# Score tiles of pooled attention as 64-row products in two halves of the TensorE array, with K's copies exchanged between the halves

## The chip, the cores and the metric

One core of one Trainium2 chip. The metric is the device time of one execution in microseconds (us); the number shown for a kernel is the median of several runs. PE is TensorE's product side, PEld its weight loads, DVE VectorE, ACT ScalarE, POOL GpSimd and SP SyncE, which issues the DMAs.

## What is computed

```python
q_pool = q.reshape(B, H, S // 2, 2, D).mean(axis=3)          # B 2, H 8, S 1152, D 64
scores = q_pool @ k.transpose(0, 1, 3, 2) / sqrt(D)
attn = softmax(scores)                                       # 576 x 1152 per head
x = concat_heads(attn @ v)                                   # 1152 x 512
out = sum_e p[:, e:e+1] * (relu(x @ w1[e]) @ w2[e])          # 4 experts, hidden 1024
```

All is float32. To stay near that accuracy with the faster fp32r products, the kernel splits an operand into hi (rounded to fp32r) and lo (the rest), and sums three terms: hi·hi, hi·lo and lo·hi.

## The kernel before

The attention stage works on eight pairs of heads, `n` = 0 to 7. A pair has nine score tiles `i` of 128 pooled queries by 1152 keys: tile `i` below 8 belongs to head `h = i % 2`, tile 8 holds the last 64 queries of both. The program is one hand-written order: block `g = 9n + i` issues, in this order on PE,

- the 18 transposes of the finished tile `g` (`T_chunk`, `pt`, 64 rows at a time, through `half_transposes` at L202),
- a part of the products with V of an older group (`PV_part`, `po`, L376),
- in some blocks a further transposition: `pr` in blocks 2 and 7 (`spread_sums`, which spreads the inverse row sums), `pk` in blocks 1 and 3 (`prep_k`, half of the next pair's K), `pq` in block 8 (`prep_q`, the q of the pair after next),
- the scores of tile `g + 3` (`S_rows`, or `S_chunk` for tile 8 and for pair 0), into a PSUM buffer of three banks of which there is one (`ps_s`). DVE sweeps it at L341 (scale, minimum, copy to SBUF), and only then may the next tile's scores be written.

From pair 1 on, tiles 0 to 7 go through `S_rows` (56 tiles). `q2` holds q hi (`z` = 0) and q lo (`z` = 1) of each head, the same in both halves of the 128 partitions. `kab` holds K of head 0 in rows 0 to 63 and of head 1 in rows 64 to 127, hi and lo apart. `k2[:, h]` holds hi and lo of head `h` one above the other, so that a 128-row product gives hi·hi + hi·lo at once. `S_rows` issues three such products at L334 (512, 512 and 128 columns), and then the lo·hi term as three 64-row products at L338: columns 0 to 511 in the upper row half, 512 to 1023 in the lower, 1024 to 1151 in the upper.

K of the pair ahead comes by these steps: the load into `kn` (L173, block 3), `join_k` on POOL (L262), which puts the two heads side by side in `kc`, transposes (`pk`), a copy to `raw` on DVE or ACT, `pool_split` on POOL (L209 hi, L210 lo) into `kab`, and `stack_k` (L274), four DMAs per call from `kab` to `k2`. `join_k(0)` stands in block 6, `join_k(1)` at the end of `prep_q` in block 8, `join_k(2)` in `prep_k`. POOL also splits the finished attention output (`finish`) and q (`prep_q`), in one queue.

After attention the expert stage runs 128-row products (L135 and L710) on 16 weight slices; the change does not touch it, save that its first products begin inside pair 7's blocks 7 and 8.

Of the kernel before, what the change touches and what calls it, by code (L numbers as in the profile page):

```python
# [8 lines left out]
F32 = mybir.dt.float32  # L9
# [8 lines left out]
def attention_moe_kernel(ctx, tc, q, k, v, probs, w1, w2, out):  # L18
    nc = tc.nc
# [3 lines left out]
    P = 128  # L23
    HALF = 64
# [11 lines left out]
    ident = const.tile([P, P], F32, name="ident")  # L36
# [18 lines left out]
    k2 = [t[:, :2 * S].rearrange("p (h s) -> p h s", h=2) for t in kk]  # L55
    kab = [t[:, 2 * S:].rearrange("p (z s) -> p z s", z=2) for t in kk]
    khl = kk[1][:, 2 * S:].rearrange("p (h t z d) -> p h t z d", h=2, t=KT, z=2)
    q2 = [q2all[:, :2304], q2all[:, 3328:]]
    stq = q2all[:, 2304:3328].rearrange("p (z s j x) -> p z s j x", z=2, s=2, j=4)
    q2m = [t[:, 2048:].rearrange("p (z x) -> p z x", z=2) for t in q2]  # L60
    q2 = [t[:, :2048].rearrange("p (z s x) -> p z s x", z=2, s=2) for t in q2]
# [77 lines left out]
    ps_t = ctx.enter_context(tc.tile_pool(name="ps_t", bufs=2, space=PSUM))  # L139
# [3 lines left out]
    with ExitStack() as actx:  # L143
# [6 lines left out]
        rb = [ap.tile([P, w], F32, name=f"rb{i}") for i, w in enumerate(GW)]  # L150
        raw = ap.tile([P, 7 * P], F32, name="raw")
        spread = ap.tile([P, 4 * HALF], F32, name="spread")
# [3 lines left out]
        pr = ap.tile([P, 2 * 9, E], F32, name="pr")  # L156
# [7 lines left out]
        NP = len(pairs)  # L164
# [27 lines left out]
        ROWS = [slice(0, HALF), slice(HALF, P)]  # L192

        def half_transposes(name, blocks, pool=None):
            if pool is None:
                pt = ps_t.tile([P, 2, 512], F32, tag="t", name=name)
            else:
                pt = pool.tile([P, 3, 512], F32, tag="s", name=name)[:, :2]
            pt = pt[:, :, :len(blocks) * HALF].rearrange("p a (k x) -> p a k x", x=HALF)
            for j, src in enumerate(blocks):  # L200
                for a, r in enumerate(ROWS):
                    nc.tensor.transpose(pt[:, a, j, :], src[r], ident[r, r])  # L202
            return pt

        def halves(t, t0, t1):
            return t[:, t0 * P:t1 * P].rearrange("p (k a x) -> p a k x", a=2, x=HALF)
# [26 lines left out]
        def half_of(h, z):  # L233
            return z if h else 1 - z
# [25 lines left out]
        def join_k(c):  # L260
            t0, t1 = KTS[c]
            nc.gpsimd.tensor_copy(  # L262
                kc[c].rearrange("p (t h d) -> p t h d", h=2, d=D), kn[:, :, t0:t1].rearrange("p h t d -> p t h d"))
# [4 lines left out]
            pool_split(ab[:, 0, cols], ab[:, 1, cols], src)  # L268

        def stack_k(n, t0, t1):  # L270
            cols, ab = slice(t0 * P, t1 * P), kab[n % 2]
            for h in range(2):
                for z in range(2):
                    nc.sync.dma_start(  # L274
                        k2[n % 2][ROWS[half_of(h, z)], h, cols].bitcast(F32), ab[ROWS[h], z, cols].bitcast(F32))

        def prep_q(n):
            pt = half_transposes("pq", [qsum[:, 2 * j:2 * j + 2].rearrange("p t d -> p (t d)") for j in range(5)] + [kc[0]])
            src = raw[:, :6 * P].rearrange("p (a k x) -> p a k x", a=2, x=HALF)
            nc.scalar.activation(src, pt, AF.Copy)  # L280
            pool_split(stq[:, 0], stq[:, 1], src[:, :, :4])
            for y in range(2):
                for half in range(2):
                    r = slice(half * HALF, (half + 1) * HALF)
                    dst = q2[n % 2].rearrange("p z s (y x) -> p (z s) y x", y=2)[r, :, y, :]
                    st = stq.rearrange("p z s j x -> p (z s) (j x)")[y * HALF:(y + 1) * HALF]
                    nc.sync.dma_start(dst.bitcast(F32), st.bitcast(F32))
            split_q2m(n, src)
            ab = kab[n % 2]
            pool_split(halves(ab[:, 0], 8, 9)[:, :, 0], halves(ab[:, 1], 8, 9)[:, :, 0], src[:, :, 5])  # L290
            if n > 1:
                join_k(1)

        def prep_k(n, c):
            t0, t1 = KTS[c]
# [17 lines left out]
        def S_chunk(g, c):  # L313
# [9 lines left out]
            for j, (w, x) in enumerate(ops):  # L323
                nc.tensor.matmul(spt[g][:, c], w, x, start=(j == 0), stop=(j == len(ops) - 1))  # L324

        def S_rows(g):
            n, i = tiles[g]
            t, h = divmod(i, 2)
            ts_ = slice(t * P, (t + 1) * P)
            sp = ps_s.tile([P, 3, 512], F32, tag="s", name="spt").rearrange("p a b -> p (a b)")[:, :S]  # L330
            spt[g] = sp.rearrange("p (c x) -> p c x", c=3)
            cs = [slice(0, 512), slice(512, 1024), slice(1024, S)]
            for c in cs:
                nc.tensor.matmul(sp[:, c], q2[n % 2][:, 0, h, ts_], k2[n % 2][:, h, c], start=True, stop=False)  # L334
            hi = [kab[n % 2][:, 0, :], k2[n % 2][:, h]]
            for a, c in ((0, cs[0]), (1, cs[1]), (0, cs[2])):
                r = ROWS[a]
                nc.tensor.matmul(sp[:, c], q2[n % 2][r, 1, h, ts_], hi[(a + h) % 2][r, c], start=False, stop=True)  # L338

        def neg_scores(g):  # L340
            nc.vector.tensor_scalar(  # L341
# [46 lines left out]
                spread.rearrange("p (c x) -> p c x", x=HALF), r[:, :4].unsqueeze(2).to_broadcast([P, 4, HALF]))  # L388

        def spread_sums(n, grp):  # L390
            pt = ps_t.tile([P, 2, 512], F32, tag="t", name="pr")[:, 0]
            r = rs[n % 2][:, 4 * grp:]
            for j in range(2):
                nc.tensor.transpose(pt[:, j * P:(j + 1) * P], spread[:, j * P:(j + 1) * P], ident)
            if grp:
                nc.tensor.transpose(pt[:, 2 * P:3 * P], r[:, 4:5].to_broadcast([P, P]), ident)
            nc.vector.tensor_copy(rb[grp][:, :256], pt[:, :256])
            if grp:
                for a, h in enumerate(ROWS):
                    nc.vector.tensor_copy(rb[1][h, 256:], pt[h, 256 + a * HALF:256 + (a + 1) * HALF])  # L400

        def split_x(op, kt, c, src, eng):
            hi, lo = xop(op, 0, kt)[:, c], xop(op, 1, kt)[:, c]
# [121 lines left out]
        for g in range(NTL):  # L525
            n, i = divmod(g, 9)
            if i == 4 and 0 < n and n + 1 < NP:
                load_kv(vn[(n + 1) % 2], v, n + 1)
            if i == 6 and n + 2 < NP:
                add_q(nc.gpsimd)  # L530
                join_k(0)
            if i == 2 and n + 2 < NP:
                load_q(n + 2)
            if g == NTL - 1:
                nc.scalar.activation(UT["m1"], chx[:, :2, :CW], AF.Copy)
            for c in range(2):
                T_chunk(g, c)
            if g <= NQT:
                exps(g + 1)
            if i == 0 and n:  # L540
                inv_sums(n - 1, 1)
            if i == 4:
                inv_sums(n, 0)
            if g == NTL - 1:
                inv_sums(n, 1)
            if NQT < g < NTL - 2 and i not in (3, 8):
                exps(g + 2)
            if g == NQT:
                PV_part(0, 1, 0, 1)
                scores(g + 2)  # L550
                exps(g + 2)
                PV_part(0, 1, 1, 3)
            else:
                pv_part(g)
            if i in SPREAD and n + SPREAD[i][0] >= 0:
                spread_sums(n + SPREAD[i][0], SPREAD[i][1])
            if g == 0:
                prep_q0()
            if n + 1 < NP:
                for fn, *args in (PREP if n else PREP0).get(i, []):  # L560
                    fn(n + 1, *args)
                if i == 8 and n + 2 < NP:
                    prep_q(n + 2)
                if i == (3 if n else 5) and n + 2 < NP:
                    load_kv(kn, k, n + 2)
            elif i == 7:
                chx = ps_s.tile([P, 3, 512], F32, tag="s", name="chx")
                for kt in range(2):
                    product(0, 0, kt, chx, True)
            elif i == 8:  # L570
                for kt in range(2):
                    product(0, 2, kt, chx, False)
            if NQT <= g < NTL - 2 and i in (3, 8):
                exps(g + 2)
            scores(g + 2 if g < NQT else g + 3)
            if g == 0:
                stack_k0()
                add_q(nc.gpsimd)
                join_k(0)
                join_k(1)  # L580
            if (n, i) == (1, 4):
                gate_weights()
            if (n, i) == (NP - 2, 4):
                load_w1(0)
            if (n, i) == (NP - 2, 7):
                w1_sums(0)
            if n == NP - 1:
                if i == 0:
                    split_x("S3", 1, slice(0, HT), xr[:, 1, :HT], nc.gpsimd)
                    load_w2(0)  # L590
                if i < 4:
                    w1_hi(0, WCH[i:i + 1])
                    w1_lo(0, WCH[i:i + 1])
                if i == 3:
                    load_w1(1)
                if i == 5:
                    w1_sums(1)
# [156 lines left out]
```

## Time and profile before

| | |
|---|---|
| median of 3 runs (lowest to highest) | 633.5 us (633.44 to 633.63) |
| the profiled execution: its own time, its span | 633.96 us, 632.1 us |
| PE busy in the span | 615.0 us (97%) |
| share of the chain that ended last on PE | 80% |
| score products, L334 and L338 (busy) | 53.2 us and 40.3 us |
| attention stage up to pair 7's last products with V | 0 to 247 us |
| chain through the expert stage's second products, L710 | 31% |

The busy times of L334 and L338 are 40.8 + 12.4 us and 28.0 + 12.3 us, 512-column and 128-column products. Busy times of PE overlap, since each product's end is modelled: its real rate is read from the starts of successive products, not from the lengths. In the timelines, neighbouring instructions of one line are merged into one row: its start is that of the first, and the start of the next row tells when the work after it began.

### The profile page before, as it was taken

The page shows a single profiled execution, that of the slowest core. Times are in us where ns is not written, and L with a number is a line of the kernel's source. Part 1 is how long each engine was busy: PE and PEld are TensorE (multiplying, and loading weights), DVE is VectorE, ACT ScalarE, POOL GpSimd, SP SyncE. Part 2 cuts the span into 40 slices and gives each one's busy share as a digit, 9 for nine tenths or more (in the row PEclk, how much of TensorE's full clock was granted, in tenths as well). Part 3 has the DMA queues.
Part 4 walks back from the last instruction along what each step waited for, and adds up shares of the span by engine and source line. Part 5 has one row for each costly group of instructions (what it writes and reads, how often), then busy time and mean ns, then how long its engine had stood idle before and what let it go on. Part 6 is the DMA issues. An engine that isn't in the chain of part 4 may idle for free.

```text
span 632.1 us, 12010 instructions
## 1 busy us (share of the span) xinstructions
PE 615.0 (97%) x4828; PEld 504.1 (80%) x4828; DVE 367.5 (58%) x571; ACT 293.9 (46%) x467; POOL 346.8 (55%) x415
## 2 busy tenths in 40 slices
PE   7899999999999999999999999999999999999997
PEld 6666666666666666889889989989989989989976
DVE  6667777777777777654454454454454454454454
ACT  5656666666666674544135135135235235235120
POOL 1654454453545498694485485485476476476040
PEclk8999999999999999999999999999999999999999
DMA  7655373736454510121121121121121121120105
GB/s 229 142 156 147 111 177 111 204 88 180 99 157 102 146 35 17 51 67 35 35 66 34 34 67 34 33 68 35 33 67 35 34 66 34 39 63 1 35 0 150
DMA packets 41783, 50.88 MB, mean 80 GB/s; under 512 B 3712, under 2 KB 27520, under 8 KB 41728
## 3 DMA queue, kind: packets, MB, share of 16 engines
q1 hardware_dynamic: 40928, 48.94, 28.0%
q10 hardware_dynamic: 800, 1.18, 0.5%
q8 instruction: 38, 0.62, 0.4%
q14 instruction: 17, 0.14, 0.1%
HBM read 30.97 MB, written 2.36 MB: 53 GB/s over the span
## 4 chain that ended last, share of the span: by engine, by line
PE 80%; POOL 8%; DVE 4%; issue 3%; ACT 2%; DMA 1%; SPq 0%; POOLq 0%; DVEq 0%; ACTq 0%
PE p L710 31%; PE chy L135 11%; PE chz L135 8%; PE chx L135 7%; PE po L376 7%; PE spt L334 4%; PE pt L202 4%; PE spt L338 3%; PE spt L324 2%; POOL q2all L210 2%; DVE sx L341 1%; DMA kq<-in_k_dram 1%; POOL q2all L209 1%; POOL xb L408 1%; PE pk L202 1%
## 5 line engine op out<-in xcount | busy, mean ns | idle before, releaser
L710 PE MATMUL p<-w2s,hb 128*128 128x512 f32 (+1 forms) x870 | 199.2, 388 | 1.1 <-DVE acc L714 0.9
L710 PEld LDWEIGHTS p<-w2s,hb 128*128 128x128 f32 x870 | 161.7, 188 | 34.3 <-issue 1.3
L714 DVE SCALAR_TENSOR_TENSOR acc<-p,pw,acc 128x512 f32<-128x512 f32 (+1 forms) x136 | 101.6, 747 | 82.7 <-PE p L710 82.7
L116 POOL TENSOR_TENSOR kk<-kq,kk 128x512 fp32r<-128x512 f32 x64 | 72.5, 1162 | 117.8 <-ACT kk L108 117.8
L341 DVE TENSOR_SCALAR_CACHE_REDUCE sx<-spt 128x1152 f32<-128x1152 f32 x72 | 97.7, 1358 | 57.7 <-PE spt L338 34.3
L347 ACT ACTIVATE sx<-sx,mn 128x1152 f32<-128x1152 f32 x72 | 90.5, 1257 | 23.6 <-DVE sx L341 23.5
L376 PE MATMUL po<-aT,vn 128*64 128x320 f32 (+1 forms) x576 | 85.5, 418 | 0.0
L641 POOL TENSOR_TENSOR hb<-xr,hb 128x576 fp32r<-128x576 f32 x48 | 68.7, 1434 | 21.9 <-ACT hb L640 21.8
L678 ACT ACTIVATE xr<-chx 128x576 f32<-128x576 f32 x15 | 9.8, 652 | 147.5 <-PE chx L135 147.5
L363 ACT ACTIVATE aT<-pt 128x640 f32<-128x640 f32 x72 | 50.6, 702 | 40.6 <-PE pt L202 40.6
L202 PEld LDWEIGHTS pt<-ident,sx 64*128 64x128 f32 x1296 | 53.8, 140 | 7.8 <-issue 3.4
L135 PE MATMUL chx<-xa,kk 128*128 128x288 f32 x384 | 56.4, 296 | 0.8 <-ACT xr L678 0.4
L202 PE MATMUL pt<-ident,sx 64*128 64x64 f32 x1296 | 56.5, 225 | 0.5 <-ACT xr L302 0.4
L135 PEld LDWEIGHTS chx<-xa,kk 128*128 128x128 f32 x384 | 53.4, 188 | 2.8 <-ACT xr L678 0.7
L376 PEld LDWEIGHTS po<-aT,vn 128*64 128x64 f32 x576 | 35.0, 136 | 20.1 <-issue 0.5
L361 DVE COPY aT<-pt 128x512 f32<-128x512 f32 x72 | 49.4, 686 | 2.4 <-PE pt L202 2.4
L95 POOL TENSOR_TENSOR kq<-kq 128x256 f32<-128x256 f32 x64 | 45.8, 738 | 7.7 <-DMA kq<-in_moe_w_dram 6.4
L639 ACT ACTIVATE xr<-xr 128x576 f32<-128x576 f32 x48 | 32.9, 686 | 34.0 <-DVE xr L637 33.9
L135 PE MATMUL chy<-xb,kk 128*128 128x288 f32 x288 | 46.6, 297 | 0.3 <-ACT xr L647 0.2
L334 PE MATMUL spt<-kk,q2all 128*128 128x512 f32 x168 | 44.1, 370 | 0.9 <-DVE sx L341 0.9
L135 PE MATMUL chy<-q2all,kk 128*128 128x288 f32 x256 | 44.1, 294 | 0.0
L617 POOL TENSOR_TENSOR w2s<-qsf,w2s 128x512 fp32r<-128x512 f32 x32 | 40.7, 1292 | 3.1 <-ACT w2s L615 3.1
(107 smaller groups left out, 757.4 us busy)
## 6 DMA issues: line engine op xcount, KB each, us to landing
kq<-in_moe_w_dram SPq DMA_DIRECT2D x64, 128.0 KB, 2.4
qsf<-in_moe_w_dram SPq DMA_DIRECT2D x16, 512.0 KB, 3.6
q2all<-q2all SPq DMA_DIRECT2D x28, 256.0 KB, 4.3
vn<-in_v_dram SPq DMA_DIRECT2D x8, 576.0 KB, 5.4
kk<-kk SPq DMA_DIRECT2D x28, 160.0 KB, 2.7
kq<-in_q_dram SPq DMA_DIRECT2D x7, 576.0 KB, 3.9
kq<-in_k_dram SPq DMA_DIRECT2D x7, 576.0 KB, 4.4
kk<-kk SPq DMA_DIRECT2D x28, 128.0 KB, 2.9
```

Of the source, the lines that this page charges most:

```text
L116: nc.gpsimd.tensor_tensor(flat(w1s[u % 2][:, 1, a:b]), flat(wf[:, a:b]), flat(w1s[u % 2][:, 0, a:b].bitcast(F32)), ALU.subtract)
L135: nc.tensor.matmul(chain[:, c, :CW], w1s[u % 2][:, a, WI[wo], kt, :], xop(xo, z, kt)[:, c * CW:(c + 1) * CW], start=(first and kt == 0 and ...
L202: nc.tensor.transpose(pt[:, a, j, :], src[r], ident[r, r])
L334: nc.tensor.matmul(sp[:, c], q2[n % 2][:, 0, h, ts_], k2[n % 2][:, h, c], start=True, stop=False)
L341: nc.vector.tensor_scalar(sx[g % 3].rearrange("p (c x) -> p c x", c=3), spt.pop(g), -INV, None, ALU.mult, ALU.min, accum_out=mn[g % 3])
L347: nc.scalar.activation(sx[g % 3], sx[g % 3], AF.Exp, bias=mn[g % 3], scale=-1.0, accum_out=sums[n % 2][:, i:i + 1])
L361: nc.vector.tensor_copy(dst, pt)
L363: nc.scalar.activation(dst, pt, AF.Copy)
L376: nc.tensor.matmul(po[h * HALF:(h + 1) * HALF, :w], vn[n % 2][:, h, kt, :], aT[grp][:, h, kt, :], start=(kt == 0), stop=(kt == KT - 1))
L641: nc.gpsimd.tensor_tensor(lo, c, hi.bitcast(F32), ALU.subtract)
L710: nc.tensor.matmul(pc, h[:, a, sl, ts_], w[:, b, sl, c0:c1], start=(m == 0), stop=(m == len(ops) - 1))
L714: nc.vector.scalar_tensor_tensor(ac, pc, pw[:, tt, e:e + 1], ac, ALU.mult, ALU.add)
```

## The change

- `S_rows` makes all three terms as 64-row products: for each term one in the upper half (columns 0 to 511) and one in the lower (512 to 1023), then the three terms of columns 1024 to 1151 in the upper half. Each column part has its own PSUM bank. Nine products a tile in place of six.
- `k2` becomes `kab` with the two row halves exchanged, so that each head's K lies in both halves: `kab` where `a == h`, `k2` elsewhere. `stack_k` issues two DMAs per call in place of four, with the same bytes; each now copies hi and lo together, and so waits for both.
- `spread_sums` uses `half_transposes`: four (blocks 7) or six (blocks 2) 64-row transposes in place of two or three 128-row ones.
- `join_k(1)` moves from the end of `prep_q` (block 8) to the start of block 7.

```diff
--- before.py
+++ after.py
@@ -268,11 +268,10 @@
             pool_split(ab[:, 0, cols], ab[:, 1, cols], src)
 
         def stack_k(n, t0, t1):
-            cols, ab = slice(t0 * P, t1 * P), kab[n % 2]
+            cols = slice(t0 * P, t1 * P)
             for h in range(2):
-                for z in range(2):
-                    nc.sync.dma_start(
-                        k2[n % 2][ROWS[half_of(h, z)], h, cols].bitcast(F32), ab[ROWS[h], z, cols].bitcast(F32))
+                nc.sync.dma_start(
+                    k2[n % 2][ROWS[1 - h], :, cols].bitcast(F32), kab[n % 2][ROWS[h], :, cols].bitcast(F32))
 
         def prep_q(n):
             pt = half_transposes("pq", [qsum[:, 2 * j:2 * j + 2].rearrange("p t d -> p (t d)") for j in range(5)] + [kc[0]])
@@ -288,8 +287,6 @@
             split_q2m(n, src)
             ab = kab[n % 2]
             pool_split(halves(ab[:, 0], 8, 9)[:, :, 0], halves(ab[:, 1], 8, 9)[:, :, 0], src[:, :, 5])
-            if n > 1:
-                join_k(1)
 
         def prep_k(n, c):
             t0, t1 = KTS[c]
@@ -323,6 +320,9 @@
             for j, (w, x) in enumerate(ops):
                 nc.tensor.matmul(spt[g][:, c], w, x, start=(j == 0), stop=(j == len(ops) - 1))
 
+        LANES = [(a, a, zq, zk) for zq, zk in ((0, 0), (0, 1), (1, 0)) for a in range(2)] + [
+            (0, 2, 0, 0), (0, 2, 0, 1), (0, 2, 1, 0)]
+
         def S_rows(g):
             n, i = tiles[g]
             t, h = divmod(i, 2)
@@ -330,12 +330,12 @@
             sp = ps_s.tile([P, 3, 512], F32, tag="s", name="spt").rearrange("p a b -> p (a b)")[:, :S]
             spt[g] = sp.rearrange("p (c x) -> p c x", c=3)
             cs = [slice(0, 512), slice(512, 1024), slice(1024, S)]
-            for c in cs:
-                nc.tensor.matmul(sp[:, c], q2[n % 2][:, 0, h, ts_], k2[n % 2][:, h, c], start=True, stop=False)
-            hi = [kab[n % 2][:, 0, :], k2[n % 2][:, h]]
-            for a, c in ((0, cs[0]), (1, cs[1]), (0, cs[2])):
+            for a, c, zq, zk in LANES:
                 r = ROWS[a]
-                nc.tensor.matmul(sp[:, c], q2[n % 2][r, 1, h, ts_], hi[(a + h) % 2][r, c], start=False, stop=True)
+                src = kab if a == h else k2
+                nc.tensor.matmul(
+                    sp[:, cs[c]], q2[n % 2][r, zq, h, ts_], src[n % 2][r, zk, cs[c]],
+                    start=(zq + zk == 0), stop=(zq == 1))
 
         def neg_scores(g):
             nc.vector.tensor_scalar(
@@ -388,16 +388,13 @@
                 spread.rearrange("p (c x) -> p c x", x=HALF), r[:, :4].unsqueeze(2).to_broadcast([P, 4, HALF]))
 
         def spread_sums(n, grp):
-            pt = ps_t.tile([P, 2, 512], F32, tag="t", name="pr")[:, 0]
             r = rs[n % 2][:, 4 * grp:]
-            for j in range(2):
-                nc.tensor.transpose(pt[:, j * P:(j + 1) * P], spread[:, j * P:(j + 1) * P], ident)
-            if grp:
-                nc.tensor.transpose(pt[:, 2 * P:3 * P], r[:, 4:5].to_broadcast([P, P]), ident)
-            nc.vector.tensor_copy(rb[grp][:, :256], pt[:, :256])
+            pt = half_transposes("pr", [spread[:, j * P:(j + 1) * P] for j in range(2)] + (
+                [r[:, 4:5].to_broadcast([P, P])] if grp else []))
+            nc.vector.tensor_copy(halves(rb[grp], 0, 2), pt[:, :, :2])
             if grp:
                 for a, h in enumerate(ROWS):
-                    nc.vector.tensor_copy(rb[1][h, 256:], pt[h, 256 + a * HALF:256 + (a + 1) * HALF])
+                    nc.vector.tensor_copy(rb[1][h, 256:], pt[h, a, 2])
 
         def split_x(op, kt, c, src, eng):
             hi, lo = xop(op, 0, kt)[:, c], xop(op, 1, kt)[:, c]
@@ -529,6 +526,8 @@
             if i == 6 and n + 2 < NP:
                 add_q(nc.gpsimd)
                 join_k(0)
+            if i == 7 and n + 2 < NP:
+                join_k(1)
             if i == 2 and n + 2 < NP:
                 load_q(n + 2)
             if g == NTL - 1:
```

What stands on PE from `pk` in block 1 to the scores in block 2 of a pair, before (`pt` transposes, `po` products with V, `pk` and `pr` as above, `spt` scores, x the count):

```order
L202 MATMUL pk<-ident,qsf 128x64 x8
L334 MATMUL spt<-kk_73,q2all 128x512 x2
L334 MATMUL spt<-kk_73,q2all 128x128
L338 MATMUL spt<-kk_73,q2all 128x512 x2
L338 MATMUL spt<-kk_73,q2all 128x128
L202 MATMUL pt<-ident,sx_92 128x64 x18
L376 MATMUL po<-aT_94,vn_89 64x320 x4
L394 MATMUL pr<-ident,spread 128x128 x2
L396 MATMUL pr<-ident,rs_105 128x128
L334 MATMUL spt<-kk_73,q2all 128x512 x2
```

and with the change:

```order
L202 MATMUL pk<-ident,qsf 128x64 x8
L336 MATMUL spt<-kk_73,q2all 128x512 x6
L336 MATMUL spt<-kk_73,q2all 128x128 x3
L202 MATMUL pt<-ident,sx_92 128x64 x18
L376 MATMUL po<-aT_94,vn_89 64x320 x4
L202 MATMUL pr<-ident,spread 128x64 x4
L202 MATMUL pr<-ident,rs_105 128x64 x2
L336 MATMUL spt<-kk_73,q2all 128x512 x6
L336 MATMUL spt<-kk_73,q2all 128x128 x3
```

The two shapes of score products, 128-row at L334 and 64-row at L338, have become one line of 64-row products, L336; and `pr` is now made by the line of the other transposes.

What stands on POOL from `join_k(0)` (`raw<-kq`) in block 6 to the end of `prep_q` in block 8, before (`xa` is the attention output's split, `q2all` that of q, `kk` that of K's last columns, `qsf<-kq` is `join_k(1)`):

```order
L262 COPY raw<-kq 128x128
L209 TENSOR_SCALAR xa<-xr 128x256
L210 TENSOR_TENSOR xa<-xr,xa 128x256
L209 TENSOR_SCALAR q2all<-raw 128x512
L210 TENSOR_TENSOR q2all<-raw,q2all 128x512
L209 TENSOR_SCALAR q2all<-raw 64x64
L210 TENSOR_TENSOR q2all<-raw,q2all 64x64
L209 TENSOR_SCALAR q2all<-raw 64x64
L210 TENSOR_TENSOR q2all<-raw,q2all 64x64
L209 TENSOR_SCALAR kk_73<-raw 128x128
L210 TENSOR_TENSOR kk_73<-raw,kk_73 128x128
L262 COPY qsf<-kq 128x512
```

and with the change:

```order
L262 COPY raw<-kq 128x128
L262 COPY qsf<-kq 128x512
L209 TENSOR_SCALAR xa<-xr 128x256
L210 TENSOR_TENSOR xa<-xr,xa 128x256
L209 TENSOR_SCALAR q2all<-raw 128x512
L210 TENSOR_TENSOR q2all<-raw,q2all 128x512
L209 TENSOR_SCALAR q2all<-raw 64x64
L210 TENSOR_TENSOR q2all<-raw,q2all 64x64
L209 TENSOR_SCALAR q2all<-raw 64x64
L210 TENSOR_TENSOR q2all<-raw,q2all 64x64
L209 TENSOR_SCALAR kk_73<-raw 128x128
L210 TENSOR_TENSOR kk_73<-raw,kk_73 128x128
```

`join_k(1)` stands ten instructions earlier, right behind `join_k(0)`.

## Rows read from the trace of the kernel before

**Rows 1.** The page, part 1: busy time, share of the span, instructions.
```profile
PE 615.0 (97%) x4828; PEld 504.1 (80%) x4828; DVE 367.5 (58%) x571; ACT 293.9 (46%) x467; POOL 346.8 (55%) x415
```

**Rows 2.** Windows, one pair of heads each: length, then busy time per engine, clock, DMA.
```profile
125.05:153.98 28.93, 28.64 (x326) 19.43 (x324) 21.74 (x39) 19.43 (x30) 13.78 (x23) 1.00 0.53 144
153.98:183.78 29.80, 28.68 (x326) 19.46 (x324) 20.78 (x39) 19.43 (x30) 15.35 (x25) 1.00 0.46 122
```

**Rows 3.** Timeline of PE, three blocks: start, length, instructions merged, idle before.
```profile
153.98 0.79 PE L334 MATMUL spt<-kk,q2all 128*128 128x512 f32 x3
154.70 0.56 PE L338 MATMUL spt<-kk,q2all 64*128 64x512 f32 x3
155.05 0.77 PE L202 MATMUL pt<-ident,sx 64*128 64x64 f32 x18
155.75 1.08 PE L376 MATMUL po<-aT,vn 128*64 128x256 f32 x8
156.76 0.44 PE L394 MATMUL pr<-ident,spread 128*128 128x128 f32 x2
156.95 0.77 PE L334 MATMUL spt<-kk,q2all 128*128 128x512 f32 x3
...
157.99 0.77 PE L202 MATMUL pt<-ident,sx 64*128 64x64 f32 x18
...
159.41 0.53 PE L202 MATMUL pq<-ident,qsf 64*128 64x64 f32 x10
...
159.93 0.50 PE L334 MATMUL spt<-kk,q2all 128*128 128x512 f32 x1
```

**Rows 4.** Timeline of PE, narrow windows: single products of one score tile.
```profile
154.32 0.39 PE L334 MATMUL spt<-kk,q2all 128*128 128x512 f32 x1
...
154.55 0.22 PE L334 MATMUL spt<-kk,q2all 128*128 128x128 f32 x1
...
155.04 0.22 PE L338 MATMUL spt<-kk,q2all 64*128 64x128 f32 x1
```

**Rows 5.** Timeline of PE around the transpositions of K for pairs 4 and 6.
```profile
107.31 1.30 PE L376 MATMUL po<-aT,vn 128*64 128x320 f32 x8
108.84 0.46 PE L202 MATMUL pk<-ident,qsf 64*128 64x64 f32 x8 [0.23 <-POOL qsf L262]
109.23 0.79 PE L334 MATMUL spt<-kk,q2all 128*128 128x512 f32 x3
...
110.99 1.30 PE L376 MATMUL po<-aT,vn 128*64 128x320 f32 x8
112.22 0.44 PE L394 MATMUL pr<-ident,spread 128*128 128x128 f32 x2
...
112.52 0.48 PE L334 MATMUL spt<-kk,q2all 128*128 128x512 f32 x1
...
167.56 0.46 PE L202 MATMUL pk<-ident,qsf 64*128 64x64 f32 x8 [1.06 <-POOL qsf L262]
```

**Rows 6.** The page, part 5: group of the expert stage's second products.
```profile
L710 PE MATMUL p<-w2s,hb 128*128 128x512 f32 (+1 forms) x870 | 199.2, 388 | 1.1 <-DVE acc L714 0.9
```

**Rows 7.** Timeline of POOL: the copy that the first of them waits for.
```profile
108.17 0.61 POOL L262 COPY qsf<-kq 128x512 f32<-128x512 f32 x1
```

**Rows 8.** Timelines of DVE and PE: one score sweep and the tiles around it.
```profile
149.08 1.36 DVE L341 TENSOR_SCALAR_CACHE_REDUCE sx<-spt 128x1152 f32<-128x1152 f32 x1
...
147.68 0.79 PE L334 MATMUL spt<-kk,q2all 128*128 128x512 f32 x3
...
150.50 0.79 PE L324 MATMUL spt<-kk,q2all 128*128 128x384 f32 x3
```

**Rows 9.** Timeline of the SP queue, and the page, part 6: issue to landing.
```profile
147.35 3.11 SPq L274 DMA_DIRECT2D kk<-kk  x4
...
q2all<-q2all SPq DMA_DIRECT2D x28, 256.0 KB, 4.3
```

**Rows 10.** Timeline of PE at the q transposition for pair 2.
```profile
42.20 0.28 PE L202 MATMUL pq<-ident,raw 64*128 64x64 f32 x2 [0.61 <-POOL raw L262]
```

## Prediction

> **What bounds the kernel now.** I read four views, from the whole to the single product. The page says that PE is busy for 615.0 us of the span [rows 1], so time can only leave through PE. The windows then show that the attention stage repeats: a pair of heads takes 28.93 us, 28.64 of them on PE, at clock 1.00, that is 2.4 GHz throughout; DVE has 21.7, ACT 19.4, POOL 13.8 [rows 2]. One pair takes 29.80 us at the same PE work, so something makes PE wait there. The timeline of PE gives what a block consists of [rows 3], and narrow windows the starts of single products [rows 4]. Starts are the measure: lengths overlap.
>
> One plain score tile reads so. The first 128-row product starts at 153.98, the second at 154.32, the third (128 columns) at 154.55, the 64-row part at 154.70, its third product at 155.04, the transposes at 155.05 [rows 3, 4]. From this I take four prices. A product of 512 columns behind another takes 0.23 us: 154.32 to 154.55, and 199.2 us for 870 in the expert stage [rows 6]. The first one takes 0.34, so a weight load that nothing hides costs 0.11. The 128-column product takes 0.15 up to the change of shape, a quarter of 0.23 (0.06) for its columns and 0.09 to drain the array. And the two 512-column products of the 64-row part take 0.34 together: a load of 0.11 and the columns of one, so the two halves run side by side and load side by side. Before the transposes, also of 64 rows, there is no drain: 0.01 us from the last product's start [rows 3, 4].
>
> Two further limits matter. DVE's sweep of the single score buffer starts at 149.08 for 1.36 us, and the next tile starts at 150.50, 2.82 after the one before at 147.68 [rows 8]: there PE waits for the sweep, in about two blocks of nine. And PE waits for POOL at `pk` [rows 5].
>
> **A plain tile.** Removed: one change of shape (0.09 drain, 0.11 load). Added: 128 column places more in the upper half, which now does three products of 512 and three of 128, and three loads more. The new tile: 0.34 for the first pair with its load, 0.23 for the second, 0.23 for the third, then three products of 128 columns in one half. The trace has no such row of three. Each needs its weights, and a load can start only when the weights before are taken up. Below lies 0.06, columns alone, were the load hidden; above 0.17, columns plus a load that nothing hides. I take the bare load, 0.11: a load of that length is 0.05 longer than the columns that could hide it. Two steps of it, and 0.01 to the transposes: 0.34 + 0.23 + 0.23 + 0.22 + 0.01 = 1.03, against 153.98 to 155.05 = 1.07. It saves 0.04 us. Where the sweep is waited for, the tile also ends 0.04 earlier, the sweep with it, and the step to the next tile shrinks by as much; so it counts there too.
>
> **A tile behind a transposition.** There are 18 behind `pk` or `pq` (six pairs: blocks 1, 3 and 8). Before, 64-row transposes were followed by 128-row products: the last transposes drained, the load lay bare. Now the shape stays: 0.09 of drain goes, and the load runs beside the last pair of transposes, some 0.06 (18 transposes take 155.05 to 155.75, less a drain, for nine pairs [rows 3]). With the tile's own 0.04 that is 0.19. The ends are 0 for the passage, if a drain and a load come in all the same, and 0.20, if both go whole; the nearest row, the same passage in the other direction at 0.01 [rows 3, 4], speaks for the upper half.
>
> **`pr`.** With two blocks it now takes 156.76 to 157.99 = 1.23 with its tile [rows 3]. New: eight transposes of `pk` take 108.84 to 109.23 = 0.39 [rows 5], less 0.09 of drain, so 0.30 for four pairs, 0.18 for two; the tile behind it without 0.06 of its load, 0.97. Together 1.15: 0.08 saved, seven times. With three blocks: 112.22 to 112.52 = 0.30 [rows 5] and 1.04 (156.95 to 157.99), together 1.34, against 0.24 + 0.97 = 1.21: 0.13 saved, seven times. In pair 7, block 7, a 128-row expert product follows `pr`: there a drain and a load come in new where none was, 0.1 lost once. DVE's copies keep their sizes.
>
> **`join_k(1)`.** At the `pk` for pair 4, 107.31 to 108.84 = 1.53 pass from the products with V; the same eight take 110.99 to 112.22 = 1.23 where nothing waits [rows 5]. The 0.30 are a wait for POOL's copy at 108.17, which stands behind the splits of q [rows 7]. This is in the blocks of pair 3; those of pairs 2 and 4 wait as long. In those of pair 5 PE's gap is 1.06 where the first shows 0.23, so the wait is 0.07 longer than the gap, 1.13. In its new place the copy is done some ten microseconds before it is needed. All of it goes, 2.0 us. What comes due next there is DVE's copy of `pk` to `raw`, which waits until POOL has split the old `raw`; behind it on DVE stands the sweep, which needs the next tile's scores, a microsecond of PE's work later, so I cost that at nothing. In the other pairs the copy was hidden before.
>
> **DMAs.** `stack_k` moves the same bytes with 28 issues in place of 56. The first copy now waits for lo as well. In the steady pairs the four are issued from 147.35 to 150.46 and first read at 153.98 [rows 3, 9]; a 256 KB copy of this kind takes 4.3 us [rows 9], so two of 320 KB, the first issued over a microsecond later, when lo is done, should land in time for the tile that reads the first, about 5 us after its issue. In pair 0 there is no such room: `pq` waits 0.61 for `join_k(0)` [rows 10], and so for the K load, which stands behind the copies in SP's queue. Two issues fewer bring that forward by about 1 us, but tile 0 of pair 1 waits for the larger copy itself. I count 0.3, between a loss of 0.5 and a gain of 0.75.
>
> **Sum.** 24 plain tiles x 0.04 = 1.0; 18 x 0.19 = 3.4; 7 x 0.08 = 0.6; 7 x 0.13 = 0.9; less 0.1; `join_k` 2.0; pair 0 0.3: **8.1 us**. The profiled execution took 633.96 us, 0.46 above the median, of which the span is 632.1. From the median, 633.5 - 8.1 = **625.4 us**. A pair of 28.93 us has three plain tiles, three behind `pk` or `pq`, one behind each kind of `pr`, and the wait of 0.30: 1.2 less, 27.7 us.
>
> **Rivals.**
> - *Short products are cheap.* If their loads are hidden, 0.10 more per tile, 56 times: 5.6, so 619.8. For it: loads run ahead of products; against it: they are longer than the columns. 0.08.
> - *The passage from transposes to scores is not free.* The weights change kind, and a drain and load stay: 18 x 0.15 and 14 x 0.15 less, 4.8, so 630.2. Against it stands the free passage the other way. 0.10.
> - *The larger copies land late.* From 5.2 us on, tile 0 of each of seven pairs waits; at 6.4 the gain is gone, 633.5. Against it: same bytes, and 4.3 us for 256 KB. 0.03.
> - *Loads lie bare within a half (slower).* Three boundaries in the upper half (second pair, third pair, first short product) each cost 0.11 more, 0.33 per tile and 18.5 in all: 643.9. It decides from 0.05 per boundary (8.1 / 56 / 3). Against it: in the old 64-row part the third product's weights were loaded while the first ran in the same half, since the two took 0.34 and not 0.45 [rows 3, 4]. 0.07. The Trainium skill ("TensorE: Matmul & The Clock Gate", Part 3, The mechanism) says that a weight load overlaps a running product only where the row group differs, which would give this rival. By that rule the 128-row products of the trace would also take 0.34 each; they take 0.23 [rows 6], so the trace disagrees.
>
> **How the numbers follow.** The forecast has 0.72. Faster: 0.72 + 0.08 + 0.10 = 0.90, same 0.03, slower 0.07; within 0.2%, 1.3 us, a measurement of this kernel can't tell a difference. The range takes in the second rival (630.2) and nearly the first: 620.0 to 630.8. The short products' upper bound, 0.06 more for each of two steps, 6.7 in all, would by itself give 632.1, just past it.
>
> **What would show it.** Right: from a plain tile's first product to the transposes 1.03 us, its second pair 0.34 and its third 0.57 after the start, short products 0.11 apart; 0.30 from the first `pk` to the scores; no wait for POOL at `pk`; pairs near 27.7 us. Wrong: pairs 0.34 apart, drains before the scores, or tiles that wait for `kk<-kk` copies.

## The result and the profile after

The changed kernel takes 628.13 us in the median of six executions, against 633.47 for the kernel before beside it: a ratio of 0.992, 95% interval 0.990 to 0.994. It is faster by 5.3 us where 8.1 were forecast; the time lies inside the range. Two later comparisons gave 628.98 and 628.01. The profile shown below is that of the first of these: its span is 625.1 us, because TensorE had the full 2.4 GHz in its first 15 us. The profiled execution of the kernel before had 0.89 of it there, and reached the part that is compared 1.9 us later.

```profile
0.00:15.00 15.00, 10.47 (x81) 8.82 (x81) 9.13 (x14) 7.34 (x12) 3.01 (x11) 0.89 0.69 225
```

That was the kernel before (windows: stretch, length, busy time and instructions of PE, PEld, DVE, ACT, POOL, granted clock, DMA share, GB/s). Of the changed kernel the same window and two pairs of heads, which answer to [rows 2], and the page's first part, which answers to [rows 1]:

```profile
0.00:15.00 15.00, 11.60 (x104) 9.73 (x104) 9.14 (x16) 8.29 (x14) 4.17 (x13) 1.00 0.66 217
121.13:149.09 27.96, 27.90 (x356) 20.27 (x354) 22.05 (x39) 19.36 (x30) 13.81 (x23) 1.00 0.55 146
149.09:177.01 27.92, 27.86 (x355) 20.23 (x353) 21.09 (x39) 19.35 (x30) 15.27 (x25) 1.00 0.53 138
```

```profile
PE 609.6 (98%) x5036; PEld 509.4 (82%) x5036; DVE 367.9 (59%) x571; ACT 294.2 (47%) x467; POOL 347.4 (56%) x415
```

A pair takes 27.94 us in place of 28.93, and the one that took 29.80 is now like the others: POOL's late copy is gone. The forecast for a pair was 27.7. Where the 5.3 us come from is read from the starts of blocks in both traces:

| stretch | before | changed | gained |
|---|---|---|---|
| from the `pr` ahead of pair 1's first tile to its second tile | 38.26 to 42.40 | 36.40 to 41.10 | -0.56 |
| on to the first tile of pair 2 | 42.40 to 67.15 | 41.10 to 65.27 | 0.58 |
| five pairs of heads, on to the first tile of pair 7 | 67.15 to 212.42 | 65.27 to 204.91 | 5.63 |
| on to the last product's start | 212.42 to 628.21 | 204.91 to 620.72 | -0.02 |

The sum is 5.63. The first two lines are a surprise: all that the tiles of pair 1 gain was lost at its first two tiles.

One plain tile of the changed kernel, from the timeline of PE (start, length, instructions, idle before), answers to [rows 3, 4]:

```profile
86.91 0.73 PE L336 MATMUL spt<-kk,q2all 64*128 64x512 f32 x4
...
87.48 0.45 PE L336 MATMUL spt<-kk,q2all 64*128 64x512 f32 x3
...
87.71 0.22 PE L336 MATMUL spt<-kk,q2all 64*128 64x128 f32 x1
87.72 0.27 PE L202 MATMUL pt<-ident,sx 64*128 64x64 f32 x1
87.77 0.27 PE L336 MATMUL spt<-kk,q2all 64*128 64x128 f32 x1
87.83 0.22 PE L202 MATMUL pt<-ident,sx 64*128 64x64 f32 x1
87.88 0.28 PE L336 MATMUL spt<-kk,q2all 64*128 64x128 f32 x1
87.89 0.27 PE L202 MATMUL pt<-ident,sx 64*128 64x64 f32 x1
...
88.00 0.36 PE L202 MATMUL pt<-ident,sx 64*128 64x64 f32 x5
...
88.66 0.44 PE L376 MATMUL po<-aT,vn 128*64 128x256 f32 x2
```

The third pair of long products starts 0.57 after the first, as forecast. The three short products of the upper half start at 87.71, 87.77 and 87.88. The transposes of the lower half do not wait for them: they begin at 87.72. Those of the upper half begin at 88.00, 1.09 after the tile's start, where 1.03 was forecast. (The rows do not name the half. The short products are all in the upper one, and nine of the 18 transposes follow each other from 88.00 on.)

The blocks with transpositions, which answer to [rows 5] and to the `pr` of [rows 3]:

```profile
68.03 0.34 PE L202 MATMUL pr<-ident,spread 64*128 64x64 f32 x4
68.18 0.99 PE L336 MATMUL spt<-kk,q2all 64*128 64x512 f32 x7
...
76.24 1.30 PE L376 MATMUL po<-aT,vn 128*64 128x320 f32 x8
77.47 0.46 PE L202 MATMUL pk<-ident,qsf 64*128 64x64 f32 x8
77.74 1.00 PE L336 MATMUL spt<-kk,q2all 64*128 64x512 f32 x7
...
78.05 0.39 PE L336 MATMUL spt<-kk,q2all 64*128 64x512 f32 x2
```

No wait for POOL stands before `pk` (1.23 from the products with V, as the undisturbed ones of [rows 5]). From `pk` to the scores 0.27 pass, where 0.39 passed before and 0.30 was forecast: the drain is gone. The load is still mostly bare: the second pair of long products starts 0.31 after the first (77.74 to 78.05), against 0.34 in the plain tile.

And the boundary of pairs 0 and 1, which answers to [rows 10], on PE and on the SP queue:

```profile
36.55 0.48 PE L336 MATMUL spt<-kk,q2all 64*128 64x512 f32 x1
37.31 1.01 PE L336 MATMUL spt<-kk,q2all 64*128 64x512 f32 x8 [0.29 <-DMA kk<-kk]
...
41.00 0.28 PE L202 MATMUL pq<-ident,raw 64*128 64x64 f32 x2 [0.92 <-POOL raw L262]
```

```profile
30.85 3.95 SPq L273 DMA_DIRECT2D kk<-kk  x4
34.85 1.00 SPq L173 DMA_DIRECT2D kq<-in_k_dram  x1
```

Pair 1's first tile has its first upper product at 36.55 and its first lower one only at 37.31, when a copy has landed. Then `pq` waits 0.92 for POOL's copy, which waits for the K load; before it was 0.61. How the two waits share the time differs between traces: in that of the first six executions, which the next expectation goes by, the tile's products are 1.34 apart (39.62 and 40.96).

### The profile page after: what moved, and what is told of

Its sections match the earlier page's. It is cut to its first block, busy times and chain, and to the rows that moved or that the text cites. A ratio compares the mean times of both kernels' runs of the same rounds, so it can differ in the third digit from the quotient of the medians.

```text
span 628.2 us, 12363 instructions
## 1 busy us (share of the span) xinstructions
PE 612.0 (97%) x5036; PEld 511.4 (81%) x5036; DVE 369.2 (59%) x571; ACT 293.4 (47%) x467; POOL 346.8 (55%) x415
## 4 chain that ended last, share of the span: by engine, by line
PE 85%; POOL 5%; DVE 4%; ACT 2%; issue 2%; DMA 1%; SPq 0%; DVEq 0%; POOLq 0%; ACTq 0%
PE p L709 31%; PE chy L135 12%; PE po L376 9%; PE spt L336 8%; PE chz L135 8%; PE chx L135 7%; PE pt L202 6%; PE spt L321 3%; DVE sx L341 1%; POOL xb L405 1%; PE pk L202 1%; POOL kk L116 1%; DMA kk<-kk 1%; PE pq L202 1%; PE pr L202 1%
## 5 line engine op out<-in xcount | busy, mean ns | idle before, releaser
L336 PEld LDWEIGHTS spt<-kk,q2all 64*128 64x128 f32 x504 | 55.2, 186 | 19.4 <-DVE sx L341 6.3
L336 PE MATMUL spt<-kk,q2all 64*128 64x512 f32 (+1 forms) x504 | 69.2, 365 | 1.8 <-DVE sx L341 0.9
L202 PE MATMUL pt<-ident,sx 64*128 64x64 f32 x1296 | 69.7, 233 | 0.5 <-ACT xr L299 0.4
L202 PEld LDWEIGHTS pt<-ident,sx 64*128 64x128 f32 x1296 | 60.0, 140 | 5.6 <-issue 3.5
```

What stands on the lines that cost most here:

```text
L336: nc.tensor.matmul(sp[:, cs[c]], q2[n % 2][r, zq, h, ts_], src[n % 2][r, zk, cs[c]], start=(zq + zk == 0), stop=(zq == 1))
```

## The experiments

Two theories. **The main one**: the 2.7 us that are missing are two mis-sized terms, the short products, whose weight loads set the end of the upper half in each of 56 tiles, and the larger copies at the boundary of pairs 0 and 1. **The rival**: the tile is paced by something else (evictions, copies, the lower half), and the boundary by POOL's order. All ratios below are to the kernel before, with 95% intervals.

**The changed kernel again.**

> The changed kernel again, beside the three that follow. Both theories: 628.1 us, 5.3 under the kernel before. The main theory puts the 2.7 us that are missing against the forecast to two terms: the upper row half's short products, whose steps are set by their weight loads (a plain tile saves 0.01 us where 0.04 was forecast, so some 1.7 us over 56 tiles), and the larger row-half copies of the second pair of heads, which land some 1.2 us later than the tiles need them. The rival puts the missing time to the end of the tile (the evictions and the transpositions' copies pace it, whatever the scores take) and to POOL's order in the first pair.

Measured: 628.98 us, 0.992 (0.990 to 0.994). Its trace is the one above.

**Four copies a call.**

```diff
-            for h in range(2):
-                nc.sync.dma_start(
-                    k2[n % 2][ROWS[1 - h], :, cols].bitcast(F32), kab[n % 2][ROWS[h], :, cols].bitcast(F32))
+            for z in range(2):
+                for h in range(2):
+                    nc.sync.dma_start(
+                        k2[n % 2][ROWS[1 - h], z, cols].bitcast(F32), kab[n % 2][ROWS[h], z, cols].bitcast(F32))
```

> The changed kernel with the row-half copies again in four transfers a call instead of two, the high parts of both heads first. Main theory: the wait of the second pair's first score tile, 1.34 us between its first upper and its first lower product, goes down to some 0.3, and the time to 626.8 to 627.2 us. Rival, the copies' size does not set the wait: 628.1 us, the wait unchanged.

Measured: 626.06 us, 0.988 (0.986 to 0.990). PE at the boundary:

```profile
36.55 0.71 PE L337 MATMUL spt<-kk,q2all 64*128 64x512 f32 x3
37.63 0.79 PE L337 MATMUL spt<-kk,q2all 64*128 64x512 f32 x6 [0.37 <-DMA kk<-kk]
...
39.64 0.53 PE L202 MATMUL pq<-ident,qsf 64*128 64x64 f32 x10
40.26 0.27 PE L202 MATMUL pq<-ident,raw 64*128 64x64 f32 x2
```

The copies matter, but not where I had said. The tile's wait only moved: the high parts come in time, and a later product waits (0.37 idle). What shrank is the wait of `pq`: its last two transposes start 0.32 after the tenth (39.94 to 40.26), against 1.15 in the changed kernel (39.85 to 41.00). In the DMA view of 28 to 48 us, K's 576 KB took 5.8 us from issue to landing behind the two-part copies and 4.1 behind the four:

```profile
kq<-in_k_dram SPq DMA_DIRECT2D x1, 576.0 KB, 5.8
```

```profile
kq<-in_k_dram SPq DMA_DIRECT2D x1, 576.0 KB, 4.1
```

It was issued 0.9 later (35.73 against 34.85), and still landed 0.8 earlier. The second tile's successor starts 0.74 earlier (43.13 against 43.87). On the SP queue of this run:

```profile
29.53 6.16 SPq L274 DMA_DIRECT2D kk<-kk  x8
35.73 0.59 SPq L173 DMA_DIRECT2D kq<-in_k_dram  x1
```

The edit changes two things at once. The copies are smaller, and the first of them no longer waits for the low parts: it is issued at 29.53, where the changed kernel issues its first at 30.85. Which of the two lets the load land sooner was not separated.

**The moved copy alone**, in the kernel before.

```diff
-            if n > 1:
-                join_k(1)
...
+            if i == 7 and n + 2 < NP:
+                join_k(1)
```

> The kernel before with one part of the change: the gathering of k's four tiles moved from the end of block 8 to the start of block 7. Main theory: seven waits of TensorE before pk, 0.30 each (0.2 in the second pair), go: 631.4 us. Rival, the wait is replaced by one for another transfer or for the score tiles' banks: 632.5 us or more.

Measured: 631.60 us, 0.997 (0.994 to 0.999), 2.1 less than before. Each pair takes 28.64 us, the one of 29.80 too: the five pairs take 143.19 in place of 145.27, which is the same 2.1. Nothing came due in its place. One of the pairs:

```profile
124.83:153.47 28.64, 28.58 (x329) 19.44 (x325) 21.75 (x39) 19.46 (x30) 13.83 (x23) 1.00 0.54 150
```

**Shorts between the long ones.**

```diff
-        LANES = [(a, a, zq, zk) for zq, zk in ((0, 0), (0, 1), (1, 0)) for a in range(2)] + [
-            (0, 2, 0, 0), (0, 2, 0, 1), (0, 2, 1, 0)]
+        LANES = [(0, 0, 0, 0), (1, 1, 0, 0), (0, 2, 0, 0), (0, 0, 0, 1), (1, 1, 0, 1), (0, 2, 0, 1),
+                 (0, 2, 1, 0), (0, 0, 1, 0), (1, 1, 1, 0)]
```

> The changed kernel with the nine products of a tile in another order: the three short ones between the long ones of the upper half, and a long one last. Main theory: the shorts' steps stay at 0.11 each, but the transpositions' first loads lie under a long product and no longer behind a short one's load, and both halves begin them together: 0.05 to 0.08 us less in each of 56 tiles, 623.5 to 625.3 us. Rival, the tile is paced by its evictions and copies: 628.1 us. If a long product behind a short one pays its whole load instead, 0.05 more for each of two, 631 us or more.

Measured: 630.73 us, 0.996 (0.994 to 0.998), nearest to the third outcome. A plain tile takes 1.78 us from its start to the products with V, 0.03 more than in the changed kernel, and a pair 28.30. The end of the upper half's products, and its transposes:

```profile
100.50 0.45 PE L336 MATMUL spt<-kk,q2all 64*128 64x512 f32 x1
...
100.79 0.40 PE L202 MATMUL pt<-ident,sx 64*128 64x64 f32 x7
```

The trace shows the price that the third outcome named. What follows a long product starts 0.28 and 0.29 after it where the long one stands behind a short one (100.05 to 100.33, 100.50 to 100.79), against 0.23 behind a long one in the changed kernel (87.48 to 87.71): 0.05 of its load lies bare, twice a tile.

**Shorts first**, a long one last.

```diff
-        LANES = [(a, a, zq, zk) for zq, zk in ((0, 0), (0, 1), (1, 0)) for a in range(2)] + [
-            (0, 2, 0, 0), (0, 2, 0, 1), (0, 2, 1, 0)]
+        LANES = [(1, 1, 0, 0), (0, 2, 0, 0), (0, 2, 0, 1), (0, 2, 1, 0), (0, 0, 0, 0), (1, 1, 0, 1),
+                 (0, 0, 0, 1), (1, 1, 1, 0), (0, 0, 1, 0)]
```

> The changed kernel with the three short products ahead of the long ones in the upper half, a long one last. Main theory, after the run with the shorts between: the upper half's steps add up to no less in any order, what the transpositions' load gains at the end is paid at the long product behind the shorts: 628 to 631 us. Rival, it was the change from long to short and back, twice a tile, that cost 0.05 each time there: with one such change less than there and the last load hidden, 625.5 to 627 us.

Measured: 629.83 us, 0.993 (0.991 to 0.996), a plain tile 1.78: the main theory's range. The long product behind the shorts pays here too: the next long one starts 0.28 after it (94.25 to 94.53). Order alone gives nothing: shorts last is the best of the three.

**One short in place of three.**

```diff
-            (0, 2, 0, 0), (0, 2, 0, 1), (0, 2, 1, 0)]
+            (0, 2, 0, 0)]
...
-                    start=(zq + zk == 0), stop=(zq == 1))
+                    start=(zq + zk == 0), stop=(zq == 1 or c == 2))
```

> The changed kernel without two of the three short products of every row-half tile (left out: the hi-lo and lo-hi terms of the last 128 keys). It measures what the short products cost. Main theory, the upper half's chain of loads sets the end of the tile: each tile loses two of its last three steps, 0.06 + 0.11 = 0.17 us between the starts of the first short product and of the third, 56 times: 618.6 us. Were each hidden but for its columns, 0.05 each: 622 us. Rival, the tile is paced by evictions and copies, or by the lower half: 626 to 628 us.

Measured: 618.96 us, 0.976 (0.974 to 0.979). A plain tile on PE, and one pair of heads:

```profile
77.29 1.02 PE L336 MATMUL spt<-kk,q2all 64*128 64x512 f32 x7
78.09 0.77 PE L202 MATMUL pt<-ident,sx 64*128 64x64 f32 x18
...
78.14 0.41 PE L202 MATMUL pt<-ident,sx 64*128 64x64 f32 x8
...
78.79 0.49 PE L376 MATMUL po<-aT,vn 128*64 128x320 f32 x2
```

```profile
120.72:147.26 26.54, 26.15 (x341) 18.49 (x337) 22.40 (x39) 19.17 (x30) 13.72 (x23) 1.00 0.57 150
```

The time is the expected one, by two errors that cancel. A plain tile takes 1.51 us where it took 1.75: 0.24 less and not 0.17, because the upper half's transposes start 0.06 after its one short product (78.08 to 78.14), and in the changed kernel 0.28 or 0.29 after the first of three. Eight tiles make 1.9 us a pair, of which 1.4 are left: PE is idle for 0.39 us in a pair where it was for 0.06. So the shorts set the end of the tile, at some 0.12 each where their columns alone would take 0.06, and the rival is out.

**The spread as 128-row products**, before 64-row scores.

```diff
-            pt = half_transposes("pr", [spread[:, j * P:(j + 1) * P] for j in range(2)] + (
-                [r[:, 4:5].to_broadcast([P, P])] if grp else []))
+            for j in range(2):
+                nc.tensor.transpose(pt[:, j * P:(j + 1) * P], spread[:, j * P:(j + 1) * P], ident)
+            if grp:
+                nc.tensor.transpose(pt[:, 2 * P:3 * P], r[:, 4:5].to_broadcast([P, P]), ident)
```

> The changed kernel with the spread of the sums again as 128-row products, before score tiles that stay of 64 rows. Main theory: the 14 blocks lose the 0.07 and 0.12 us that the trace of the changed kernel shows there (7 x 0.065 + 7 x 0.117 = 1.3), and the scores' first load lies bare behind the change of shape, up to 0.06 more in each: 629.4 to 630.2 us. Rival, the change of shape only moves from before pr to behind it and nothing else differs: 628.1 us.

Measured: 631.84 us, 0.998 (0.996 to 1.000), about twice the cost that I expected. Two and three blocks on PE:

```profile
71.46 0.44 PE L394 MATMUL pr<-ident,spread 128*128 128x128 f32 x2
71.83 1.02 PE L336 MATMUL spt<-kk,q2all 64*128 64x512 f32 x7
...
84.36 0.44 PE L394 MATMUL pr<-ident,spread 128*128 128x128 f32 x2
84.64 0.27 PE L396 MATMUL pr<-ident,rs 128*128 128x128 f32 x1
84.84 1.02 PE L336 MATMUL spt<-kk,q2all 64*128 64x512 f32 x7
```

Two blocks take 0.37 to the scores, against 0.15 (68.03 to 68.18) as 64-row products and 0.19 in the kernel before [rows 3]. I had taken the change of shape for one that only moves. It does not: from the start of the products with V to `pr` 1.015 us pass whether `pr` has 64 rows or 128, since those products have a shape of their own. So the change of shape behind `pr` is a new one: blocks 7 and 2 are 0.25 and 0.30 longer than in the changed kernel, 3.8 for seven of each.

**K's load ahead of the second call's copies**, with four copies a call.

```diff
+                if n == 0 and i == 5:
+                    load_kv(kn, k, 2)
                 for fn, *args in (PREP if n else PREP0).get(i, []):
                     fn(n + 1, *args)
...
-                if i == (3 if n else 5) and n + 2 < NP:
+                if n and i == 3 and n + 2 < NP:
```

> The changed kernel with four copies a call (as in the run above that had them) and K's load for the third pair issued ahead of the copies of the second call. Main theory: what TensorE waits for at the boundary of the first two pairs is bytes, some 1.3 MB that have to land in one stretch, and their order decides who waits: the wait of pq, 0.31 us, goes, and the first score tile of the second pair waits longer, by 0.5 or more: 626.0 to 627.0 us. Rival, the copies have room and the load does not: 625.7 us.

Measured: 630.80 us, 0.996 (0.994 to 0.998), slower than either rival said. The order does decide who waits: `pq` waits no more, and the tile waits much longer. But the price is larger, for what follows in the windows:

```profile
39.51 0.50 PE L337 MATMUL spt<-kk,q2all 64*128 64x512 f32 x2 [1.45 <-DMA kk<-kk]
40.75 1.23 PE L337 MATMUL spt<-kk,q2all 64*128 64x512 f32 x6 [0.73 <-DMA kk<-kk]
```

```profile
38.00:40.00 2.00, 0.55 (x3) 0.19 (x2) 0.25 (x1) 0.67 (x2) 0.84 (x2) 1.00 1.06 281
40.00:42.00 2.00, 1.27 (x14) 1.16 (x14) 0.00 (x0) 0.00 (x0) 0.00 (x0) 0.72 0.08 22
42.00:44.00 2.00, 2.00 (x23) 1.13 (x20) 1.89 (x3) 1.19 (x2) 0.00 (x0) 0.50 0.00 0
```

PE did 0.55 us of work in 2, and behind that the granted clock was 0.72 and then 0.50, that is 1.2 GHz, while PE was busy again.

**Four copies, again, and the copy put back**, beside the changed kernel.

> The changed kernel, beside the two that follow: 628 us by either theory.

> The version with four copies a call, run again beside the changed kernel itself. Main theory: 0.8 us less than the changed kernel, all of it at the pq of the first two pairs. Rival, the first run of it was low by chance: the same as the changed kernel within 0.3 us.

> The changed kernel with the gathering of k's four tiles put back to the end of block 8. Main theory, the parts add up: 2.1 us more than the changed kernel, 630.1 us, and the wait of 0.30 before pk in six pairs back again, the one of the fifth pair longer by 0.8 or so. Rival, with the shorter tiles pk comes sooner and waits longer for the same copy, 0.3 to 0.5 us more in each pair: 632 us or more.

Measured: the changed kernel 628.01 (0.992; 0.990 to 0.994), four copies 626.02 (0.988; 0.986 to 0.990), the copy put back 630.38 (0.996; 0.994 to 0.998). Four copies are better a second time, by 2.0 us. The two traces that were compared show 0.8 of it (583.5 against 584.3 us from the boundary on); the traces of this second pair show 0.35 (583.51 against 583.86 from the first score product of pair 1). Where the rest lies is open. It is not the clock of the first microseconds: of the executions with a mean granted clock of 0.999 or more, the nine of the changed kernel have a median of 628.0 us and the nine with four copies one of 626.0. The copy put back costs 2.4, and its waits before `pk` are these:

```profile
104.77 1.30 PE L378 MATMUL po<-aT,vn 128*64 128x320 f32 x8
106.47 0.46 PE L202 MATMUL pk<-ident,qsf 64*128 64x64 f32 x8 [0.40 <-POOL qsf L262]
...
161.59 1.30 PE L378 MATMUL po<-aT,vn 128*64 128x320 f32 x8
164.09 0.46 PE L202 MATMUL pk<-ident,qsf 64*128 64x64 f32 x8 [1.21 <-POOL qsf L262]
```

1.70 pass to `pk` where 1.23 would, so each of three waits is 0.47, not the 0.30 of [rows 5], and the fourth 1.28: there are four such pairs, not six. POOL is no faster, so shorter tiles only wait longer. The parts do not quite add up: beside shorter tiles the moved copy is worth a little more.

## Why the prediction was right, and which terms were off

The direction, the mechanism and the range held. Term by term, from the mean block times of both traces:

| term | forecast | measured |
|---|---|---|
| 24 plain tiles | 1.0 | 24 x (1.762 - 1.751) = 0.3 |
| 18 behind `pk` or `pq` | 3.4 | 12 x (2.156 - 2.002) + 6 x (2.278 - 2.102) = 2.9 |
| `pr`, two blocks | 0.6 | 7 x (1.935 - 1.870) = 0.5 |
| `pr`, three blocks | 0.9 | 7 x (2.044 - 1.936) = 0.8 |
| expert product behind `pr` | -0.1 | -0.1 |
| `join_k(1)` | 2.0 | 2.1 (alone) |
| the last `pr`, ahead of the expert stage | not counted | 0.476 - 0.325 = 0.15 |
| pair 0 | 0.3 | -0.8 |

The measured column adds up to 5.85. The traces show 5.63; the stretch from the first products with V behind the last `pr` (250.93 before, 243.10 changed) is 0.3 longer than before (377.6 against 377.3), for which I have no cause; with the moved copy alone it takes 377.5. The medians show 5.3.

**The plain tile was mis-sized.** The step that failed is "Two steps of it, and 0.01 to the transposes". By the starts, the 0.01 belongs to the half that has no short product. In the kernel before, one transpose starts with the short product at 155.04 [rows 4], the next ones 0.06 later:

```profile
155.10 0.41 PE L202 MATMUL pt<-ident,sx 64*128 64x64 f32 x8
```

(The row is of a narrow window, which holds eight.) Nine of the 18, those of the half with the short product, follow each other from there, and the tile ends with them. It is the same in the run with one short product (78.08, 78.14). So there are three steps from the first short product to the upper half's transposes, 0.06, 0.11 and 0.11 or 0.12, in all 0.28 to 0.29, and the forecast had two of 0.11 and one of 0.01. Compared in the upper half, its transposes start 1.090 after a plain tile's start where it was 1.115 before (means), a gain of 0.025 and not 0.04; and from the first to the last of them 0.509 pass where 0.494 did. What is left is 0.01. So 0.03 us a tile are missing, in the tiles behind transpositions and `pr` too: 56 x 0.03 = 1.7.

That the shorts are paced by their loads and not by their columns is right, and the run with one short takes the first rival away: shorts are not cheap. A bare load costs 0.11 with 64 rows as with 128: 0.34 pass to the second long product in both kernels, where a hidden load leaves 0.23. The Trainium skill ("TensorE: Matmul & The Clock Gate", Part 2, LDWEIGHTS (loading the stationary operand)) has a load's time by its columns, whatever its rows; by its formula 128 columns are an estimate of 107 ns. The 0.11 of the scores in both traces agrees. The transposes do not: their loads have 128 columns too, and in one half they follow each other at 0.06 us (nine in 0.494 to the last one's start).

**Pair 0 was mis-sized, and its sign was wrong.** "Two issues fewer bring that forward by about 1 us" counted issues on SP's queue. The issue of K's load did come forward, by 0.9 against pair 1's first tile (34.85 against 36.55, before 37.64 against 38.45), but behind larger copies, which start later since they wait for the low parts, the load took 5.8 us to land, and POOL and `pq` waited for it. Before:

```profile
37.64 0.59 SPq L173 DMA_DIRECT2D kq<-in_k_dram  x1
```

The first tile's block is 0.35 longer and the one with `pq` 0.17 longer; with the 0.07 and 0.18 that these two should have gained, that is 0.8. The run with four copies gives 0.74 of it back.

**What held.** `join_k(1)`: 2.1, alone, with all its waits, and nothing late in its place. The passage from transposes to scores: some 0.14 of the 0.15 forecast is gained, though from the drain more than from the load, so the second rival is out. The larger copies in the steady pairs: no tile waits for them after pair 1, so the third rival came true at one boundary of seven. In the whole trace the larger copies take 4.2 and 4.0 us in the median for 320 and 256 KB, close to the 4.3 of [rows 9]. And the rival on loads that lie bare within a half is out: the third long product starts 0.57 after the first, one step of 0.34 and one of 0.23, as in [rows 4]; a bare load at each would make it 0.68.

**What the changes of shape were worth.** The spread of the sums looked like a small part, 1.5 forecast and 1.3 measured. The run that puts it back shows 3.8: with the scores in halves, the old spread costs 2.5 more than this part was seen to gain. That is no contradiction: the two parts of the change need each other.

## What to carry to other kernels

Here a chain of products whose columns take 0.06 us was paced by weight loads of 0.11. Price every step of such a chain, up to the start of what stands behind it, and when two halves of the array run side by side, read that start in the half that ends last. Fewer, larger DMAs saved issues here, but the load behind them landed later: look at what lands in the same stretch, and at what each transfer waits for, not only at what is issued. And parts of a change are worth different sums alone and together: here, what removes a change of shape was worth more where the neighbours had the new shape already.

## What the runs showed of the hardware that was not expected

- Products of the lower half overtake products of the upper half that stand before them in the program. In program order the three short products stand ahead of all transposes; in the trace the first transpose starts at 87.72, ahead of the second and third short product (87.77 and 87.88). The Trainium skill ("TensorE: Matmul & The Clock Gate", Part 3, The mechanism) says that products start and end in program order. For products in different row halves these starts disagree.
- In the run with K's load ahead, the granted clock fell to half behind a stretch in which PE worked for 0.55 of 2 us, and stayed there while PE worked without a gap (42 to 44 us). The 18 transposes behind it took 1.22 us where they take 0.72, and the products with V 1.05 where they take 0.72, so the wait cost nearly one microsecond more than it lasted.
- The order of long and short products in one half matters by 0.03 us a tile. Behind a short product a long one is followed 0.05 us later than behind a long one, in both of the other orders; with the shorts last no long product stands behind one.
- Not tried: one of the three short products in the lower half, which ends earlier. Both halves would then write one PSUM bank, and the starts above show no order between the halves.
